# A three-stage attention and two-MLP kernel: warm-up matmuls planned with two activity levels, weight loads moved to GpSimd's queue

## The chip, the cores and the metric

The program runs on one core of a Trainium2 chip. The metric is device microseconds of one execution; the kernel before takes 969.86 us, the median of three runs (968.71 to 970.83). TensorE (PE in the profile) is the matrix engine, VectorE (DVE) and ScalarE (ACT) work on vectors, SyncE (SP) issues DMAs, and GpSimd (POOL) does nothing before but set four constants.

## The reference

Inputs are q, k, v of 4 batches, 8 heads, 576 positions and head size 64. The attention output is the sum of two softmax attentions: one on means over groups of 4 positions, and one in a band of 7 positions:

```python
out_d = sm_attn(q_d, k_d, v_d)                 # 144 pooled positions, dense
out_up = np.repeat(out_d, factor, axis=2)      # factor = 4
mask = np.abs(pos[:, None] - pos[None, :]) < factor
scores = np.where(mask, scale * np.matmul(q, k.transpose(0, 1, 3, 2)), -1e9)
out_local = softmax(scores) @ v
x = (out_up + out_local)                       # as 2304 tokens x 512
h = x @ w_in;  g = np.maximum(h, 0) + alpha * np.minimum(h, 0);  x = g @ w_out
h = x @ w_in2; g = np.where(h > 0, h, np.exp(np.minimum(h, 0)) - 1); out = g @ w_out2
```

Both MLPs are 512 to 2048 to 512. The weights arrive as 64-bit floats, and every MLP product is computed as three products of high and low parts.

## The kernel before, in words

The program is written out by a planner that runs when the kernel is built. It keeps a small clock of its own (class `_Clock`: an estimated time for each engine, and how many columns TensorE has streamed in each stretch of `TICK`), and it lets some hundred generator threads (`th_...`) place their next instruction when the estimated times allow it. What comes out is one fixed instruction order for each engine. The chip runs each engine's list in order and waits by semaphores; the estimates play no part there. All instructions pass through the helper at L231, so every row of the profile reads L231 and the tiles tell what it is.

The MLP runs in slots. A slot is one group of 288 tokens (384 in layer 2) and one block `f` of 128 hidden units: 12 matmuls with the input weights `wi` (`mm_in`), then the activation (`n`, `r`, `gh`, `gl`), then 12 matmuls with the output weights `wo` (`out1`). The first run of slots, 0 to 9, is group 0 with `f` = 0 to 9; slots 10 to 25 are group 1 with all 16 blocks; 26 to 31 finish group 0. Before a weight block can be used, it is loaded raw (512 KB, tile `raw`), and converted by two ACT and four DVE instructions (`cp`, `cw`, `wi` or `wo`); in layer 1, this is `th_conv(1, k)` for the 32 blocks in the order wi0, wo0, wi1, and so on.

The attention of batch 0, first half of the positions, comes before slot 0: banded blocks per pair of heads (`th_dense`, tiles `dP`), pooled attention (`P`, `pt`, `od`), the sum `x`, and its parts `xh` and `xl`. The second half (u = 1) follows while the slots already run, and it goes through DRAM: the score blocks `ss` are written to `scr`, their band is read back as `s`, a softmax on DVE gives `a`, which is written to the diagonal of `pscr` and read back as `pp`; TensorE transposes `pp` and multiplies it with `vb`. Batch 1 goes the same way in two halves. `pscr` holds zeros first, from two DMAs of 702 KB. `xsp` is a copy of x in DRAM.

All DMAs are issued by SP, in one order. The weight loads of layer 1 come from `th_ldw(1)`: load k waits in the planner until block k - 4 is converted (`PF`), and for the tiles whose memory it takes over. `run_while` is where the planner has nothing to place: it moves its time on by 100 ns, and when `quiet()` says that TensorE has streamed too few columns in the present stretch it places a warm-up matmul (tile `warm`, 128x128 by 256 columns, its result unused).

Of the kernel before, what the change touches and what calls it, by code (L numbers as in the profile page):

```python
# [7 lines left out]
F32 = mybir.dt.float32  # L8
# [9 lines left out]
NP = H // 2  # L18
# [19 lines left out]
T0 = 600.0  # L38
QB, QK = 64, 70
QO = 0, 64, 128, 192, 224  # L40
MORE = 1.0
LIM, EARLY, ECONV, DLA = 1300.0, 700.0, 200.0, 2000.0
PB, FB, RB, PF, CS = 1000.0, 300.0, 300.0, 4, 6
OS, OP, OPS, OSD, OSO, OAV, OX = 5, 15, -8, 6, 0, 10, -5
# [11 lines left out]


class _Clock:
    TICK, BUSY = 10240 / 3, 2640.0
    LAG = {("ACT", "DVE"): 142.0, ("ACT", "PE"): 194.0, ("ACT", "SP"): 145.0, ("DVE", "ACT"): 128.0,  # L60
           ("DVE", "DVE"): 127.0, ("DVE", "PE"): 179.0, ("DVE", "SP"): 120.0, ("PE", "ACT"): 197.0,
           ("PE", "DVE"): 196.0, ("PE", "SP"): 189.0, ("DMA", "SP"): 900.0, ("DMA", "ACT"): 907.0,
           ("DMA", "DVE"): 907.0, ("DMA", "PE"): 1003.0, ("ACT", "ACT"): 140.0}
    MANY = {"ACT": 70.0, "DVE": 93.0, "SP": 50.0, "PE": 0.0}

    def __init__(self):
        self.cols = {}
        self.t = dict.fromkeys(("PE", "ACT", "DVE", "SP", "DMA"), 0.0)
        self.t["SP"] = 560.0
        self.hw = 0.0  # L70
        self.seen = {}
        self.share = 1.0
        self.uses, self.bar, self.slots, self.count = {}, {}, {}, {}
        self.cur = self.ctx()
# [5 lines left out]
    def pe(self, t, cost, share):  # L80
        k = int(t / self.TICK)
        while cost > 0.0:
            slow = 1.0 if self.cols.get(k - 1, 0.0) >= self.BUSY else 2.0
            part = min(cost, ((k + 1) * self.TICK - t) / slow)
            self.cols[k] = self.cols.get(k, 0.0) + part * 2.4 * share
            t, cost, k = t + part * slow, cost - part, k + 1
        return t

    def quiet(self):
        k = int(self.t["PE"] / self.TICK)  # L90
        return self.cols.get(k, 0.0) < MORE * self.BUSY

    def span(self, ap):
        dims = [(abs(int(a)), int(n)) for a, n in ap.ap]
# [21 lines left out]
    def deps(self, eng, outs, ins):  # L116
# [13 lines left out]
        for src, e in last.items():  # L130
            if e > self.seen.get((eng, src), 0.0):
                self.seen[eng, src] = e
                n += 1
                t = max(t, e + self.LAG.get((src, eng), 0.0))
        return t + (self.MANY[eng] if n > 1 else 0.0)

# [26 lines left out]
            n, want = n * k, want * k  # L163
        return n * (8 if ap.dtype == U64 else 4)

    def dma(self, out, in_):
        outs, ins = [self.span(out)], [self.span(in_)]
        n = int(out.shape[0]) * _free(out) * (8 if out.dtype == U64 else 4)
        piece = min(self.run(out), self.run(in_))
        cost = max(n / 360 * (2 if piece < 512 else 1), n / piece / 16 * 7)  # L170
        self.t["SP"] = max(self.t["SP"], self.deps("SP", outs, ins))
        self.hw = max(self.hw + 25, self.t["SP"]) + 450
        end = max(self.t["DMA"], self.hw + 650) + cost
        self.t["DMA"] = end
        self.note("DMA", outs, ins, end)
        c = self.cur
        c["t"] = max(c["t"], end + 900)
        c["on"] = "DMA"


def _free(ap):
    n = 1
    for d in ap.shape[1:]:
        n *= int(d)
    return n


class _Engine:
# [31 lines left out]
    def __getattr__(self, op):  # L220
        fn = getattr(self.eng, op)

        def call(*args, **kw):
            if op == "dma_start":
                self.clock.dma(kw["out"], kw["in_"])
            else:
                outs = [kw[k] for k in ("out", "accum_out") if k in kw] + list(args[:1])
                ins = [a for k, a in kw.items() if k not in ("out", "accum_out") and hasattr(a, "ap")]
                wait = 0.6 * int(kw["lhsT"].shape[1]) if op == "matmul" else 0.0
                self.clock.op(self.name, *self.cost(op, kw, args), outs, ins + list(args[1:]), wait)  # L230
            return fn(*args, **kw)  # L231
        return call
# [3 lines left out]
def fused_kernel(ctx: ExitStack, tc: tile.TileContext, qk, vt, vl, ql, kl, vb, w_in1, w_out1, alpha,  # L236
                 w_in2, w_out2, ident_d, mask_d, zero_d, vd, maskd_d, out):
    nc = tc.nc
    ck = _Clock()
    PE, ACT, DVE, SP = (_Engine(n, e, ck) for n, e in  # L240
                        (("PE", nc.tensor), ("ACT", nc.scalar), ("DVE", nc.vector), ("SP", nc.sync)))

    const = ctx.enter_context(tc.tile_pool(name="const", bufs=1))
    wp = ctx.enter_context(tc.tile_pool(name="w", bufs=1))
# [10 lines left out]
    maskb = const.tile([128, 5, QK], BF16, name="maskb")  # L255
    identb = const.tile([128, 128], BF16, name="identb")
    warm = const.tile([128, 4], BF16, name="warm")

    W = {}
    raw = {}  # L260
# [51 lines left out]
    wsrc = {(1, "i"): w_in1, (1, "o"): w_out1, (2, "i"): w_in2, (2, "o"): w_out2}  # L312

    def load_w(key):
        ly, nm, f = key
        if wide:
            raw[key] = wp.tile([128, 512], U64, tag=f"w{nm}{f}", name=f"raw{nm}{f}")
            SP.dma_start(out=raw[key], in_=wsrc[ly, nm][f])

    gs = {}  # L320
    cp = {}
# [19 lines left out]
    st = {}  # L341
# [408 lines left out]
    def finish(*key):  # L750
        done[key] = ck.cur["t"]
# [80 lines left out]
    def run_while(cond):  # L832
        while cond():
            now[0] = max(now[0], ck.t["PE"])
            while not (cons() | pe(RB)) and cond():
                now[0] += 100
                while WARM and keep[0] is not None and ("S", 0, NP - 1, 0) in done and ck.t["PE"] < now[0] - 50 and ck.quiet():
                    at(now[0] - 100)
                    PE.matmul(out=keep[0][:, 0:256], lhsT=warm[:, 0:1].to_broadcast([128, 128]),
                              rhs=warm.unsqueeze(1).to_broadcast([128, 64, 4]),  # L840
                              start=True, stop=True)
                assert now[0] < 5e6, [(t["p"], t["w"]) for t in threads]
# [4 lines left out]
    def fill(budget):  # L847
        now[0] = max(now[0], ck.t["PE"])
        cons()
        pe(budget)  # L850

    def tick():
        sync()
        pe(PB)
        ck.cur = ck.ctx()
# [370 lines left out]
    def th_ldw(ly):  # L1226
        for k, it in enumerate(items):
            if ly == 2:
                yield "key", "fr", (2,) + it
            else:  # L1230
                if PT0 <= k < PP0:
                    yield "key", "pav", 0, k - PT0, 0
                elif PP0 <= k < V0:
                    yield "key", "pav", 0, k - PP0, 0
                elif V0 <= k < SH0:
                    yield "key", "sv", 0, k - V0
                elif k >= QK0:
                    yield "key", "dav", (k - QK0) // 2, (1,)
                    for u in range(2):
                        yield "key", "smm", 0, (k - QK0) // 2, u  # L1240
                if k >= PF:
                    yield "key", "cv", 1, k - PF
            yield ("DMA",)
            load_w((ly,) + it)
            finish("ld", (ly,) + it)
            ck.cur["t"] = now[0]
# [185 lines left out]
    with tc.manual_schedule():  # L1432
# [32 lines left out]
        spawn(th_soft0(0, 1), -10, 0)  # L1465
        spawn(th_vb(0, 1), UV, 0)
        spawn(th_ldw(1), 0)
        for k in range(2 * NF):
            spawn(th_conv(1, k), k / CS, early=ECONV)
# [29 lines left out]
        for s in range(NS1 + NS2):  # L1499
            slot[0] = s if s else -1  # L1500
            ly, g, f, first, last, i = seq[s]
# [3 lines left out]
            if s == T7:  # L1505
                assert all(t["p"] < -50 for t in threads), [t["w"] for t in threads]
                pA.__exit__(None, None, None)
                pC = tc.tile_pool(name="pC", bufs=1)
                cp["pool"] = pC.__enter__()
                tokens.update({"x2": [0.0], "x2s": [0.0, 0.0], "cp": [0.0] * 2, "cw": [0.0] * 2, "os": [0.0] * 4})  # L1510
                spawn(th_ldw(2), 0)
                for k in range(2 * NF):
                    spawn(th_conv(2, k), 2 + k / 100)
                for gg in range(NG2):
                    spawn(th_x2(gg), gg)
# [5 lines left out]
            key = (ly, "i", f)  # L1521
# [124 lines left out]
```

## Time and profile before

| | |
|---|---|
| median of 3 runs | 969.86 us (968.71 to 970.83) |
| the profiled execution | 970.52 us, span 968.7 us |
| busy, share of the span | PE 97%, LDWEIGHTS 89%, DVE 62%, ACT 49%, POOL 0% |
| mean granted clock | 0.974 |
| warm-up matmuls | 60 |
| DMA | 86.17 MB, one queue in use by the program |

The profile gives an instruction's start from the first instruction's; "granted clock" is the share of full speed that TensorE was given in a stretch, 1.00 for 2.4 GHz and 0.50 for 1.2 GHz. Matmul durations overlap, so a busy PE is not at its peak. Times on SP are those of issuing a DMA, not of its landing.

### The profile page before, as it was taken

How to read it: one execution, taken by the hardware profiler on the slowest of the kernel's cores; microseconds unless marked ns; L12 is line 12 of the kernel's file. 1: busy time of each engine (PE TensorE's matmuls, PEld its weight loads, DVE VectorE, ACT ScalarE, POOL GpSimd, SP SyncE). 2: the span in 40 equal slices, each digit the busy share in tenths (PEclk: the TensorE clock that was granted, in tenths of full speed). 3: DMA queues.
4: the chain of work that ended last, by engine and by line, in shares of the span. 5: the costliest groups of instructions: out<-in, count | busy, mean ns of one | idle time of the engine just before them, and what ended most of it. 6: DMA issues, size and time to landing. Idle time of an engine off the chain costs nothing.

```text
span 968.7 us, 16336 instructions
## 1 busy us (share of the span) xinstructions
PE 938.5 (97%) x6428; PEld 866.0 (89%) x6428; DVE 599.5 (62%) x1253; ACT 471.3 (49%) x1200; POOL 0.2 (0%) x4
## 2 busy tenths in 40 slices
PE   5978999899999999999999999999999999999998
PEld 3767889799999899999999999989999999998997
DVE  5778998645959789899638999732322322322222
ACT  5575678555432572332326677644443433433433
POOL 0000000000000000000000000000000000000000
PEclk9687999989999999999999999999999999999999
DMA  9277762534111523100207950003100100000000
GB/s 291 93 247 228 240 222 52 102 110 160 50 31 54 167 70 90 33 19 37 82 1 238 377 195 33 1 1 98 55 12 1 66 1 1 33 1 1 33 1 32
DMA packets 60933, 86.17 MB, mean 89 GB/s; under 512 B 29279, under 2 KB 40415, under 8 KB 60599
## 3 DMA queue, kind: packets, MB, share of 16 engines
q1 hardware_dynamic: 60857, 85.14, 28.0%
q8 instruction: 50, 0.82, 0.4%
q14 instruction: 26, 0.21, 0.1%
HBM read 69.93 MB, written 16.63 MB: 89 GB/s over the span
## 4 chain that ended last, share of the span: by engine, by line
PE 89%; DMA 6%; ACT 2%; DVE 2%; issue 1%; SPq 1%; ACTq 0%
PE bank L231 89%; DMA scr<-ss 2%; DMA s<-scr 1%; DMA qk<-in_qk_dram 1%; DMA pp<-pscr 1%; DMA pscr<-a 1%; SPq L231 1%; ACT dP L231 0%; DVE cw L231 0%; ACT ss L231 0%; ACT cp L231 0%; ACT P L231 0%; DVE s L231 0%; ACT n L231 0%; DVE cp L231 0%
## 5 line engine op out<-in xcount | busy, mean ns | idle before, releaser
L231 PE MATMUL bank<-xh,wi 128*128 128x288 f32 x1024 | 240.6, 304 | 3.6 <-DVE wi L231 2.8
L231 ACT ACTIVATE n<-bank 128x288 f32<-128x288 f32 (+1 forms) x224 | 99.4, 444 | 290.7 <-PE bank L231 290.5
L231 PE MATMUL bank<-gh,wo 128*128 128x288 f32 x1024 | 237.1, 302 | 1.2 <-ACT ys L231 1.2
L231 PE MATMUL bank<-x2h,wi 128*128 128x384 f32 x768 | 211.2, 337 | 0.0
L231 PEld LDWEIGHTS bank<-xh,wi 128*128 128x128 f32 x1024 | 176.4, 191 | 8.6 <-DVE wi L231 3.9
L231 PEld LDWEIGHTS bank<-gh,wo 128*128 128x128 f32 x1024 | 174.4, 190 | 6.3 <-issue 2.9
L231 PE MATMUL bank<-wo,gh 128*128 128x512 f32 x576 | 179.0, 392 | 0.0
L231 DVE SCALAR_TENSOR_TENSOR r<-n,bank 128x384 f32<-128x384 f32 x96 | 53.1, 554 | 195.0 <-ACT n L231 194.9
L231 ACT ACTIVATE gh<-r 128x288 fp32r<-128x288 f32 (+1 forms) x224 | 106.8, 477 | 100.2 <-DVE r L231 99.7
L231 PE MATMUL bank<-xl,wi 128*128 128x288 f32 x512 | 152.9, 299 | 0.0
L231 PE MATMUL bank<-gl,wo 128*128 128x288 f32 x512 | 151.8, 297 | 0.0
L231 DVE TENSOR_TENSOR gl<-r,gh 128x288 fp32r<-128x288 f32 (+1 forms) x224 | 111.4, 498 | 60.8 <-ACT gh L231 59.2
L231 PEld LDWEIGHTS bank<-x2h,wi 128*128 128x128 f32 x768 | 140.3, 188 | 3.9
L231 PE MATMUL bank<-x2l,wi 128*128 128x384 f32 x384 | 128.9, 336 | 0.0
L231 PEld LDWEIGHTS bank<-wo,gh 128*128 128x128 f32 x576 | 106.8, 188 | 18.2
L231 PE MATMUL bank<-wo,gl 128*128 128x512 f32 x288 | 113.8, 395 | 0.0
L231 DVE SCALAR_TENSOR_TENSOR r<-n,nal,bank 128x288 f32<-128x288 f32 x128 | 65.2, 509 | 53.1 <-ACT n L231 52.5
L231 PEld LDWEIGHTS bank<-xl,wi 128*128 128x128 f32 x512 | 98.0, 191 | 0.0
L231 PEld LDWEIGHTS bank<-gl,wo 128*128 128x128 f32 x512 | 97.3, 190 | 0.0
L231 PEld LDWEIGHTS bank<-x2l,wi 128*128 128x128 f32 x384 | 72.1, 188 | 3.8
L231 PEld LDWEIGHTS bank<-wo,gl 128*128 128x128 f32 x288 | 54.0, 187 | 11.5
L231 ACT ACTIVATE n<-n 128x384 f32<-128x384 f32 x96 | 50.4, 525 | 3.1
(101 smaller groups left out, 895.6 us busy)
## 6 DMA issues: line engine op xcount, KB each, us to landing
rawi<-in_w_in_dram SPq DMA_DIRECT2D x32, 512.0 KB
rawo<-in_w_out_dram SPq DMA_DIRECT2D x32, 512.0 KB
qk<-in_qk_dram SPq DMA_DIRECT2D x12, 582.0 KB
yT<-ys SPq DMA_DIRECT2D x32, 144.0 KB
out_dram<-os SPq DMA_DIRECT2D x18, 256.0 KB
vl<-in_vl_dram SPq DMA_DIRECT2D x4, 960.0 KB
vv<-in_vt_dram SPq DMA_DIRECT2D x12, 288.0 KB
kls<-in_kl_dram SPq DMA_DIRECT2D x12, 288.0 KB
```

The lines of the kernel that those rows point to most:

```text
L231: return fn(*args, **kw)
```

## The change

The planner's model of TensorE's clock gets a memory. Before, a stretch was taken as slow when the stretch before it had fewer than `BUSY` (2640) columns. Now a fast stretch stays fast at `BUSY` columns, a slow one becomes fast only after `RISE` (3500), and the first `FREE` (6) stretches are taken as fast; `quiet()` asks for warm-ups up to the level of the present state. The weight loads are issued by GpSimd, and the limit of four loads ahead of the conversions is dropped in favour of one wait: before its first load GpSimd copies one column of the last `v` tile of batch 0, which makes it wait until that tile has landed.

```diff
 class _Clock:
-    TICK, BUSY = 10240 / 3, 2640.0
+    TICK, BUSY, FREE, RISE = 10240 / 3, 2640.0, 6, 3500.0
...
     def pe(self, t, cost, share):
         k = int(t / self.TICK)
         while cost > 0.0:
-            slow = 1.0 if self.cols.get(k - 1, 0.0) >= self.BUSY else 2.0
+            slow = 1.0 if self.fast(k) else 2.0
...
+    def fast(self, k):
+        while len(self.gear) <= k:
+            n = len(self.gear)
+            need = self.BUSY if n and self.gear[-1] else self.RISE
+            self.gear.append(n < self.FREE or self.cols.get(n - 1, 0.0) >= need)
+        return self.gear[k]
+
     def quiet(self):
         k = int(self.t["PE"] / self.TICK)
-        return self.cols.get(k, 0.0) < MORE * self.BUSY
+        return self.cols.get(k, 0.0) < (self.BUSY if self.fast(k) else self.RISE)
...
-    def dma(self, out, in_):
+    def dma(self, out, in_, eng="SP"):
...
+        if eng == "SP":
+            self.hw = max(self.hw + 25, self.t["SP"]) + 450
+            end = max(self.t["DMA"], self.hw + 650) + cost
+        else:
+            self.t[eng] += 1000
+            end = max(self.t["DMA"], self.t[eng] + 650) + cost
...
-            SP.dma_start(out=raw[key], in_=wsrc[ly, nm][f])
+            GP.dma_start(out=raw[key], in_=wsrc[ly, nm][f])
...
-                if k >= PF:
-                    yield "key", "cv", 1, k - PF
+                if not k:
+                    yield "key", "ldv", NP - 1
+                    nc.gpsimd.tensor_copy(out=pace, in_=st["vv", 0, NP - 1][:, 0:1])
```

Since the planner places everything by its estimates, the order on all engines shifts. Warm-up matmuls are 52 instead of 60: 30 before slot 0 (22 before), 8 between slots 0 and 1 (10), 9 after slot 1 (18), 5 later (10).

PE, before, between the transposes of batch 0's banded blocks (`dP_197` is pair 1, `dP_220` pair 2; bank_71 takes the warm-ups):

```order
L231 MATMUL bank_72<-ident,dP_197 70x128 x4
L231 MATMUL bank_69<-ident,dP_197 70x128
L231 MATMUL bank_73<-ident,dP_220 70x128 x4
L231 MATMUL bank_66<-ident,dP_220 70x128
L231 LDWEIGHTS warm
```

PE, now, at the same place (`dP_166` is pair 0, `dP_206` pair 1, `dP_257` pair 2):

```order
L241 MATMUL bank_72<-dP_166,vd_124 64x64 x8
L241 MATMUL bank_72<-dP_166,vd_124 64x32 x2
L241 MATMUL bank_73<-ident,dP_206 70x128 x4
L241 MATMUL bank_67<-ident,dP_206 70x128
L241 LDWEIGHTS warm
L241 MATMUL bank_71<-warm 128x256
```

The last two rows come three times before the transposes of `dP_257` follow. So the product of pair 0's block with `vd` has moved up ahead of the later transposes, and three warm-ups stand between two pairs that adjoined.

SP, before, from the last loads of batch 0 to the second half's band `s_777`:

```order
L231 DMA vd_141<-in_vd_dram 70x640
L231 DMA rawi_230<-in_w_in_dram 128x512
L231 DMA rawo_273<-in_w_out_dram 128x512
L231 DMA rawi_275<-in_w_in_dram 128x512
L231 DMA rawo_288<-in_w_out_dram 128x512
L231 DMA rawi_485<-in_w_in_dram 128x512
L231 DMA xsp<-x 128x1152
L231 DMA mask<-in_mask_dram 128x182
L231 DMA pscr_98<-in_zero_dram 12x14982
L231 DMA pscr_97<-in_zero_dram 12x14982
L231 DMA scr_1_94<-ss 72x624 x2
L231 DMA rawo_592<-in_w_out_dram 128x512
```

SP, now, from the same load on:

```order
L241 DMA vd_142<-in_vd_dram 70x640
L241 DMA xsp<-x 128x1152
L241 DMA mask<-in_mask_dram 128x182
L241 DMA pscr_99<-in_zero_dram 12x14982
L241 DMA pscr_98<-in_zero_dram 12x14982
L241 DMA scr_1_95<-ss 72x624 x4
L241 DMA s_784<-scr_1_95 72x32x7
L241 DMA pscr_99<-a 72x32x7
L241 DMA pp<-pscr_99 72x624 x4
L241 DMA vb<-in_vb_dram 78x2048
```

The weight loads are gone from between, and so are, before the band is read, the loads of `vb`, `qk` and `vv`. GpSimd, which had no such rows before, now has all 64 loads; its list begins so:

```order
L1255 COPY pace<-v_3_138 128x1
L241 DMA rawi_292<-in_w_in_dram 128x512
L241 DMA rawo_294<-in_w_out_dram 128x512
L241 DMA rawi_319<-in_w_in_dram 128x512
L241 DMA rawo_332<-in_w_out_dram 128x512
L241 DMA rawi_349<-in_w_in_dram 128x512
L241 DMA rawo_370<-in_w_out_dram 128x512
```

Eight loads have nothing to wait for but the copy; the next eight wait for the products of batch 0's banded blocks, whose memory they take, and loads 25 to 32 for the pooled attention of the second half.

SP, before, in batch 1 (`pscr_97` holds the first half, `pscr_98` the second; `s_2264` is the second half's band):

```order
L231 DMA pscr_97<-a 72x32x7
L231 DMA s_2264<-scr_1_96 72x32x7
L231 DMA pp<-pscr_97 72x624
L231 DMA scr_1_92<-ss 72x4x78
L231 DMA qk<-in_qk_dram 128x1164
L231 DMA vv<-in_vt_dram 128x576
L231 DMA pp<-pscr_97 72x624
L231 DMA pscr_98<-a 72x32x7
L231 DMA pp<-pscr_97 72x624
```

SP, now, at that place (`pscr_98` is the first half, `pscr_99` the second, `s_2192` the second half's band):

```order
L241 DMA scr_1_97<-ss 72x624
L241 DMA s_2192<-scr_1_97 72x32x7
L241 DMA qk<-in_qk_dram 128x1164
L241 DMA vv<-in_vt_dram 128x576
L241 DMA pscr_98<-a 72x32x7
L241 DMA pscr_99<-a 72x32x7
L241 DMA pp<-pscr_98 72x624
```

Both halves' softmax results are now written before the first `pp` is read. On DVE the conversions keep their places: the tenth `wi` has nine `wo` ahead of it in both orders, and the band's softmax of batch 0 stands after the fourth `wi` in both.

## Rows read from the trace of the kernel before

**Rows 1.** Page, busy us, share of the span and instructions by engine.

```profile
PE 938.5 (97%) x6428; PEld 866.0 (89%) x6428; DVE 599.5 (62%) x1253; ACT 471.3 (49%) x1200; POOL 0.2 (0%) x4
```

**Rows 2.** Windows: stretch, length, busy us by engine, granted clock, DMA share, GB/s.

```profile
21.40:41.90 20.50, 20.11 (x171) 14.62 (x171) 15.52 (x40) 10.59 (x39) 0.00 (x0) 0.50 0.17 65
52.10:55.50 3.40, 3.40 (x27) 2.64 (x26) 1.90 (x5) 3.37 (x13) 0.00 (x0) 0.50 0.82 266
69.20:72.60 3.40, 3.40 (x26) 2.56 (x26) 3.23 (x11) 2.69 (x10) 0.00 (x0) 0.50 0.36 84
76.00:89.60 13.60, 11.11 (x67) 10.14 (x67) 10.17 (x19) 6.65 (x16) 0.00 (x0) 0.50 0.82 251
89.60:182.00 92.40, 90.17 (x809) 83.87 (x809) 81.40 (x166) 66.41 (x183) 0.00 (x0) 1.00 0.53 162
192.00:198.90 6.90, 5.09 (x25) 5.12 (x26) 1.80 (x5) 4.28 (x15) 0.00 (x0) 0.51 0.57 170
198.90:960.00 761.10, 760.43 (x4902) 712.87 (x4902) 443.98 (x912) 338.48 (x791) 0.00 (x0) 1.00 0.20 64
```

**Rows 3.** Chain that ended last: start us, us, what.

```profile
23.37 18.55 PE bank L231 x157
...
54.52 7.38 DMA scr<-ss
...
61.97 5.31 DMA s<-scr
...
70.84 6.27 DMA pscr<-a
77.13 2.73 DMA pp<-pscr
...
79.91 21.98 PE bank L231 x206
```

**Rows 4.** Waits of PE, 41.9 to 110 us: us, times, longest.

```profile
PE bank L231 <- DVE wi L231: 2.8, 4, 1.1
...
PE bank L231 <- DMA pp<-pscr: 2.3, 1, 2.3
```

**Rows 5.** Timeline of PE: the last wait for converted weights.

```profile
109.25 0.54 PE L231 MATMUL bank<-xh,wi 128*128 128x288 f32 x2 [1.07 <-DVE wi L231]
```

**Rows 6.** Windows of DVE alone: busy us, granted clock, DMA share, GB/s.

```profile
5.30:41.00 35.70, 26.30 (x73) 0.73 0.54 174
41.00:67.30 26.30, 19.38 (x43) 0.92 0.84 270
67.30:109.20 41.90, 36.87 (x75) 0.80 0.74 231
```

**Rows 7.** The same windows for warm-up instructions alone, 21.4 to 41.9 us.

```profile
21.40:41.90 20.50, 5.22 (x19) 2.33 (x19) 0.00 (x0) 0.50 0.17 65
```

**Rows 8.** SP's timeline: start, us to issue, what.

```profile
15.55 0.33 SPq L231 DMA_DIRECT2D rawi<-in_w_in_dram  x1
40.06 0.33 SPq L231 DMA_DIRECT2D xsp<-x  x1
...
185.19 4.20 SPq L231 DMA_DIRECT2D pp<-pscr  x1
```

**Rows 9.** Windows: DMA at full rate, and DMA idle.

```profile
17.07:20.48 3.41, 2.33 (x19) 1.41 (x16) 3.24 (x12) 2.98 (x17) 0.00 (x0) 1.00 1.02 362
27.31:30.72 3.41, 3.41 (x38) 2.23 (x35) 2.76 (x9) 1.36 (x7) 0.00 (x0) 0.50 0.00 0
```

**Rows 10.** Groups by line and form, 0 to 110 us: busy us, mean ns.

```profile
L231 DVE TENSOR_SCALAR cp<-cp 128x512 uint32<-128x512 uint32 x21 | 8.8, 419 | 0.0
```

**Rows 11.** Timeline of PE, 180 to 194 us: batch 1's blocks `pp`.

```profile
183.34 0.78 PE L231 MATMUL bank<-ident,pp 72*78 72x72 f32 x8 [0.99 <-DMA pp<-pscr]
...
189.99 0.67 PE L231 MATMUL bank<-ident,pp 72*78 72x72 f32 x8 [0.96 <-DMA pp<-pscr]
...
193.81 1.15 PE L231 MATMUL bank<-ident,pp 72*78 72x72 f32 x8 [2.30 <-DMA pp<-pscr]
```

More of the change, by code (lines that the diff above doesn't have):

```diff
@@ L40 @@
 QO = 0, 64, 128, 192, 224
-MORE = 1.0
 LIM, EARLY, ECONV, DLA = 1300.0, 700.0, 200.0, 2000.0
@@ L63 @@
            ("DMA", "DVE"): 907.0, ("DMA", "PE"): 1003.0, ("ACT", "ACT"): 140.0}
-    MANY = {"ACT": 70.0, "DVE": 93.0, "SP": 50.0, "PE": 0.0}
+    MANY = {"ACT": 70.0, "DVE": 93.0, "SP": 50.0, "PE": 0.0, "GP": 50.0}
     def __init__(self):
-        self.cols = {}
-        self.t = dict.fromkeys(("PE", "ACT", "DVE", "SP", "DMA"), 0.0)
+        self.cols, self.gear = {}, []
+        self.t = dict.fromkeys(("PE", "ACT", "DVE", "SP", "DMA", "GP"), 0.0)
         self.t["SP"] = 560.0
@@ L170, in dma @@
         cost = max(n / 360 * (2 if piece < 512 else 1), n / piece / 16 * 7)
-        self.t["SP"] = max(self.t["SP"], self.deps("SP", outs, ins))
-        self.hw = max(self.hw + 25, self.t["SP"]) + 450
-        end = max(self.t["DMA"], self.hw + 650) + cost
+        self.t[eng] = max(self.t[eng], self.deps(eng, outs, ins))
+        if eng == "SP":
[4 more added lines that the diff above has]
+            end = max(self.t["DMA"], self.t[eng] + 650) + cost
         self.t["DMA"] = end
@@ L224, in call @@
             if op == "dma_start":
-                self.clock.dma(kw["out"], kw["in_"])
+                self.clock.dma(kw["out"], kw["in_"], self.name)
             else:
@@ L239, in fused_kernel @@
     ck = _Clock()
-    PE, ACT, DVE, SP = (_Engine(n, e, ck) for n, e in
-                        (("PE", nc.tensor), ("ACT", nc.scalar), ("DVE", nc.vector), ("SP", nc.sync)))
+    PE, ACT, DVE, SP, GP = (_Engine(n, e, ck) for n, e in
+                            (("PE", nc.tensor), ("ACT", nc.scalar), ("DVE", nc.vector), ("SP", nc.sync),
+                             ("GP", nc.gpsimd)))
     const = ctx.enter_context(tc.tile_pool(name="const", bufs=1))
@@ L257, in fused_kernel @@
     warm = const.tile([128, 4], BF16, name="warm")
+    pace = const.tile([128, 1], F32, name="pace")
     W = {}
```

## The prediction

> **What bounds the kernel now.** I read the page's busy shares first, then windows with the granted clock, the chain, PE's waits, and DVE alone. PE is busy 97% of the span [rows 1]. From 198.9 us on it is busy 760.43 of 761.10 us at full clock, and from 89.6 to 182 us 90.17 of 92.40 [rows 2]. Neither part has anything to give, so what this change can win or lose lies before 89.6 us and between 182 and 199 us. There the granted clock falls to 0.50, which is 1.2 GHz, four times, for 20.5, 3.4, 3.4 and 13.6 us, and once more for 6.9 us [rows 2].
>
> A slow PE alone is not the bound, though. In the slots up to 9, PE waits for converted weights four times, the last time at 109.25 us [rows 4, 5]: there the conversions on DVE set the pace. DVE's ledger is therefore the one to keep. From 5.3 us to the last `xl` of slot 0 at 41.0 us it works 26.3 of 35.7 us (9.4 idle); to the band's softmax at 67.3 us 19.4 of 26.3 (6.9 idle); to the tenth `wi` at 109.2 us 36.9 of 41.9 (5.0 idle) [rows 6]. Its work in these three parts is the same after the change, since the order keeps the conversions' places. The kernel can become faster by as much of the 21.3 us of idle time as goes, until PE is the bound by itself.
>
> **The change part by part.**
>
> *A, warm-ups before slot 0.* From 23.4 us the chain is PE alone for 18.55 us [rows 3], at half clock although PE was busy 20.11 of 20.50 us; 5.22 us of that were 19 warm-ups, 0.27 us each, and they did not bring the clock back for 20 us [rows 2, 7]. Real work was 14.9 us at half clock, so 7.5 at full. The 30 warm-ups now cost 30 x 0.14 = 4.2 us at full clock. With the clock held PE needs 11.7 us where DVE needs 15.5 [rows 2], so DVE becomes the bound and the stretch shrinks by at most 20.5 - 15.5 = 5.0 us. With the clock not held, eight more warm-ups at 0.27 us cost 2.2 us. The warm-ups now stand closer together and the planner asks more of a slow stretch, so I lean to the first and take a gain of 4 us: DVE will still wait on ACT and PE somewhere.
>
> *B, the band's way through DRAM.* Before, SP's queue is the weights' queue too. The fourth `scr` write took 7.38 us from issue to landing and the read of `s` 5.31 [rows 3]; `vb` and weights were issued just ahead. Now nothing but the chain's own DMAs stands there. Against that, loads no longer pause: before, the DMA engines stood still between 24 and 40 us, when `xsp` was at the head of SP's queue [rows 8, 9]; now GpSimd issues on as memory comes free. A load takes 512 KB / 362 GB/s = 1.45 us at the rate of [rows 9], so 24 loads fill 35 us from about 18 us on, and run into the `scr` and `s` transfers of 44 to 67 us. Between all 6.9 us of idle time gone and 5 us lost (the price is worked out with the rivals), I take a gain of 2 us, nearest to the queueing that the 7.38 us show over the 5.31.
>
> The trace has one program queue, so it shows no sharing between two. The Trainium skill, "DMA: Bandwidth & Descriptors", sections "Issuing engines are not separate DMA queues" and "Queues, rings and completion order", says that transfers issued by different engines run on the same 16 DMA engines, which take packets from their queues in turn, and that a second issuer saves issue time alone. By that, B alone gives nothing or a loss, and the total would be 2 us higher; no run here shows it yet.
>
> *C, up to the tenth `wi`.* From 76 to 89.6 us PE ran at half clock, busy 11.11 us, after waiting for `pp` for 2.3 us [rows 2, 4]; at full clock that is 5.6 us. DVE idles 5.0 us in this part. Bounds are 0 and 5.0; I take 3, since the second half's `x` sums stand some ten us of DVE work further back now, which covers the read of `pp`.
>
> *D, batch 1.* PE waits 0.99, 0.96 and 2.30 us for three `pp` blocks [rows 11], and the clock is low for 6.9 us after it, of which 5.09 busy [rows 2]: 4.2 + 2.5 = 6.7 us lost. In the new order there are 21 more MLP matmuls between the last score blocks and the first `pp`; at 761.1 us / 4902 = 0.155 us they cover 3.3 us. But both halves' `pscr` writes now stand ahead of the first `pp`, and before, the read behind the second write took 4.20 us to issue [rows 8] and landed 8.6 us after its issue. One long wait replaces three short ones. Bounds: 6.7 gained, 4 lost (8.6 less 3.3, less the 0.99 that the first wait was); I take 0.
>
> *E, issuing on GpSimd.* No row shows its cost. SP's issues take from 0.33 us to 4.20 [rows 8]. The tenth `wi` is load 19: at 0.33 us an issue nothing waits, at 4.2 us it goes out at 18 + 80 = 98 us, too late by some us for its conversion. I go by the lower end, since the long issue stood in a queue full of small pieces. What it can disturb is DVE. The copies `cp` take 0.419 us [rows 10]; 24 loads that each hold one up by its length would cost 10 us, loads that hold up none cost 0. `cp` fills 8.8 of 110 us, so a random load meets one in 8% of cases: 24 x 0.08 x 0.42 = 0.8 us. I take 1 us lost, which is near the lower end because most of DVE's instructions here are of other forms.
>
> The Trainium skill, "SBUF - State Buffer", section "SBUF: two separate sides", holds that DVE and GpSimd lock each other out of a shared port for a whole instruction when DVE runs in a two-port mode, and that loads issued from GpSimd then wait for their descriptors. By that rule the loads are late by up to one `cp` each, which the earlier start covers; the sum by it is the same to 1 us.
>
> *The rest.* Layer 2's 32 loads move to GpSimd too; PE there is busy all the time [rows 2] and I price them at nothing. If that cover were gone, PE would wait as in [rows 5], 1 us a block.
>
> Sum: 4 + 2 + 3 + 0 - 1 = 8 us off the profiled execution's 970.5 us, 962.5; that execution lies 0.7 us above the median of 969.86, so 962.
>
> **The rivals.** *All of it comes.* The clock holds, the chain is early, and D goes too: 5.0 + 6.9 + 5.0 of DVE's idle time, limited by PE's own needs to about 11, and 6 from D: 953. For it speaks that PE has 20 us at half clock to give before 89.6 us; against it that DVE's waits on ACT and PE are many and small. Chance 0.15.
>
> *The clock does not hold.* The warm-ups don't do what they are for: PE falls to half clock near 21 us again and stays there until slot 0. A costs 2 us, B and C give 3 to 4 at most since the weights are there earlier: 969. For it: 19 warm-ups in a stretch that was busy 98% left the clock low. Chance 0.18.
>
> *The loads crowd out the band.* This is the slower side, one mechanism: 24 loads (35 us) and the chain's own 2.8 MB (by the tiles' sizes 576 KB of `xsp`, 91 of mask, 1404 of zeros, 704 of `scr`; at 362 GB/s 8 us) begin at 18 us, so the DMA engines have work until 61 us. The band's read is 2304 pieces of 28 bytes (72 x 32 runs in the order), and before it took 5.31 us with little beside it. If its pieces wait in turn with whole weight rows it can't end before the loads do; with `vb` and later loads behind that it lands near 72 instead of 67.3 us, DVE stands still in front of its softmax, PE idles, the clock falls, and A's gain is lost there. The `pp` reads suffer in the same way: 974. It decides from the landing of `s`: later than 68 us and the change loses. For it: the DMA engines were busy 0.84 of this part already [rows 6]. Chance 0.22.
>
> **How the numbers follow.** My forecast, 962, has 0.45, with a range of its own of 956 to 968. A measurement of this kernel can tell about 0.2%, 1.9 us, from no change. Faster than that (below 967.9): nearly all of the forecast, the first rival and a third of the second: 0.43 + 0.15 + 0.06 + 0.02 = 0.66. Slower (above 971.8): most of the third and a fifth of the second: 0.19 + 0.04, 0.23. The same: 0.11. The range reaches from a little below the first rival to the third: 951 to 975.
>
> **What would show it.** A: no stretch at 0.50 longer than two of the short ones between 21 us and slot 0, and slot 0's last `xl` near 37 us. B: `s` lands near 61 us; DMA never idle between 18 and 55 us. C: the tenth `wi` at about 100 us. D: one wait for `pp` of 3 to 6 us instead of three. E: `cp` on DVE at 0.42 us, or longer. The forecast is wrong if `xl` comes after 40 us, if the band's softmax begins after 65 us, or if PE idles for more than 8 us in batch 1.

## The result, and the profile after

| | before | after |
|---|---|---|
| median | 969.71 us (968.71 to 970.83, 4 runs) | 980.59 us (980.01 to 982.46, 4 runs) |
| the profiled execution | 970.52 us | 980.49 us, span 978.7 us |

The ratio is 1.0122, with a 95% interval of 1.0104 to 1.0139: the changed kernel is slower by 10.9 us, where 962 was forecast with a range up to 975.

The page's busy time by engine (us, share of the span, instructions), to be held against [rows 1]:

```profile
PE 935.1 (96%) x6429; PEld 864.4 (88%) x6429; DVE 598.7 (61%) x1253; ACT 472.8 (48%) x1200; POOL 35.1 (4%) x69
```

PE is busy 3.4 us less than before in a span that is 10.0 us longer: the loss is idle time. The windows of the changed kernel, with the columns of [rows 2], cut where its granted clock changes:

```profile
32.90:39.70 6.80, 6.59 (x49) 5.04 (x47) 4.58 (x9) 3.39 (x8) 2.39 (x5) 0.50 0.41 126
53.40:60.20 6.80, 6.45 (x31) 5.76 (x32) 5.89 (x11) 4.87 (x13) 2.58 (x5) 0.50 1.00 390
70.45:94.35 23.90, 12.66 (x67) 10.86 (x68) 17.00 (x38) 12.17 (x32) 2.37 (x4) 0.50 0.54 123
94.35:182.00 87.65, 87.27 (x806) 81.05 (x804) 80.11 (x167) 65.58 (x182) 0.00 (x0) 1.00 0.38 101
189.90:200.20 10.30, 9.48 (x57) 8.36 (x58) 3.90 (x8) 3.23 (x9) 0.00 (x0) 0.50 0.48 123
200.20:960.00 759.80, 757.38 (x4917) 710.50 (x4915) 443.91 (x912) 342.15 (x806) 17.53 (x32) 1.00 0.21 66
```

Before slot 0 the clock is low for 6.8 us instead of 20.5. How short that stretch is differs between executions: of the nine traces with this same list of PE (this one and eight of the experiments below), three have some 6.8 us there and six some 13.6, the changed kernel's second trace (e12) among them, while the two with the planning of before (e2, e9) have 20.5. From e12:

```profile
28.00:41.50 13.50, 11.53 (x82) 8.37 (x79) 10.35 (x24) 6.95 (x21) 4.69 (x9) 0.50 0.67 226
```

So the warm-ups shorten it, but not always by as much as this trace shows. From 70.45 us on the clock is low for 23.9 us, and PE is busy half of that. In sum no clock is won: the stretches at 0.50 shown here add up to 47.8 us, and those of [rows 2] do too. What comes before the 23.9 us is in the chain that ended last, the DMA pieces of 40 to 80 us (start us, us, what):

```profile
41.60 10.15 DMA scr<-ss
...
54.91 5.57 DMA scr<-ss
60.61 13.36 DMA s<-scr
```

The read of `s` went out 1.4 us earlier than in [rows 3] and took 13.36 us instead of 5.31. It was the same read, 2304 pieces of 28 bytes; what had changed was beside it. The DMA queues from 60 to 74 us (packets, MB, share of the 16 engines' time):

```profile
q0 software_dynamic: 1004, 3.61, 70.0%
q1 hardware_dynamic: 2316, 0.06, 9.7%
```

q0 holds GpSimd's weight loads, q1 the band. 0.06 MB of the band spread over the time of 3.61 MB of weight rows. GpSimd's timeline shows where these came from (start, us to issue):

```profile
17.10 0.18 POOL L1255 COPY pace<-v 128x1 f32<-128x1 f32 x1 [16.66 <-DMA v<-in_vt_dram]
17.22 0.66 POOL L241 DMA_DIRECT2D rawi<-in_w_in_dram  x1
...
59.06 0.53 POOL L241 DMA_DIRECT2D rawi<-in_w_in_dram  x1 [1.00 <-PE bank L241]
60.95 0.53 POOL L241 DMA_DIRECT2D rawo<-in_w_out_dram  x1 [1.35 <-DMA rawi<-in_w_in_dram]
64.04 0.53 POOL L241 DMA_DIRECT2D rawi<-in_w_in_dram  x1 [2.57 <-PE bank L241]
64.66 0.53 POOL L241 DMA_DIRECT2D rawo<-in_w_out_dram  x1
```

Nine of its loads go out between 51.33 and 64.66 us, in the middle of the band's way. What the late band does to DVE and PE, as their waits from 40 to 110 us (us, times, longest), DVE first:

```profile
DVE s L241 <- DMA s<-scr: 10.7, 1, 10.7
```

```profile
PE bank L241 <- ACT P L241: 9.5, 1, 9.5
PE bank L241 <- ACT ss L241: 3.5, 1, 3.5
PE bank L241 <- DMA pp<-pscr: 2.8, 1, 2.8
```

DVE stands in front of the band's softmax for 10.7 us, since its list is fixed. Work of the pooled attention is queued behind it, so PE stands 9.5 us for `P`, and meanwhile the clock falls. DVE alone, in the stretches of [rows 6], and then the tenth `wi`:

```profile
5.30:41.00 35.70, 28.50 (x77) 0.90 0.86 288
...
41.00:67.30 26.30, 17.92 (x39) 0.87 0.99 375
...
67.30:109.20 41.90, 31.68 (x67) 0.71 0.57 152
```

```profile
112.25 0.68 DVE L241 SCALAR_TENSOR_TENSOR wi<-cw,wi 128x512 fp32r<-128x512 f32 x1
```

DVE has done 2.2 us more work by 41 us than in [rows 6], but idles 10.2 instead of 5.0 us in the third part; the tenth `wi` is ready at 112.9 instead of 109.2 us. SP's timeline gives the rest:

```profile
36.90 0.35 SPq L241 DMA_DIRECT2D xsp<-x  x1
...
60.61 0.31 SPq L241 DMA_DIRECT2D s<-scr  x1
77.25 0.30 SPq L241 DMA_DIRECT2D pscr<-a  x1
83.62 9.78 SPq L241 DMA_DIRECT2D pp<-pscr  x4
93.45 0.36 SPq L241 DMA_DIRECT2D vb<-in_vb_dram  x1
```

And in batch 1 PE's timeline has one long wait where [rows 11] have three short ones:

```profile
190.72 1.15 PE L241 MATMUL bank<-ident,pp 72*78 72x72 f32 x8 [4.55 <-DMA pp<-pscr]
```

### The profile page after: what moved, and what is told of

Its sections match the earlier page's. It is cut to its first block, busy times and chain, and to the rows that moved or that the text cites. A ratio compares the mean times of both kernels' runs of the same rounds, so it can differ in the third digit from the quotient of the medians.

```text
span 978.7 us, 16380 instructions
## 1 busy us (share of the span) xinstructions
PE 935.1 (96%) x6429; PEld 864.4 (88%) x6429; DVE 598.7 (61%) x1253; ACT 472.8 (48%) x1200; POOL 35.1 (4%) x69
## 4 chain that ended last, share of the span: by engine, by line
PE 46%; issue 45%; DMA 4%; DVE 2%; ACT 2%; SPq 0%; POOL 0%; POOLq 0%; ACTq 0%; DVEq 0%
PE bank L241 46%; DMA scr<-ss 2%; DMA s<-scr 1%; ACT dP L241 1%; DMA yT<-ys 1%; ACT P L241 1%; DMA rawi<-in_w_in_dram 0%; DVE cw L241 0%; DMA ident<-in_ident_dram 0%; DVE qk L241 0%; DVE wi L241 0%; ACT ss L241 0%; DVE cp L241 0%; ACT cp L241 0%; DVE x L241 0%
## 5 line engine op out<-in xcount | busy, mean ns | idle before, releaser
L241 PE MATMUL bank<-xh,wi 128*128 128x288 f32 x1024 | 244.8, 307 | 4.1 <-ACT wi L241 2.1
```

## The experiments

Theory "crowding": the loads on the second queue share the DMA engines with the band's small pieces. Rivals: the new instruction order itself costs the time ("order"), issuing from GpSimd does ("GpSimd"), or the missing limit of four does ("limit"). The experiments ran on other chips, where the kernel before took 964.4 to 965.1 us (medians, single runs 958.7 to 969.8). So ratios to the kernel before, taken in the same runs, are compared, not times.

| run | loads from, limit in the planner, what else | ratio | 95% interval |
|---|---|---|---|
| e12_after | GpSimd, no limit: the changed kernel again | 1.0118 | 1.0094 to 1.0141 |
| e1_clock_only | SP, limit | 0.9965 | 0.9947 to 0.9983 |
| e16_clock_again | the same | 0.9972 | 0.9952 to 0.9992 |
| e6_one_queue | SP, no limit | 1.0072 | 1.0048 to 1.0097 |
| e2_pool_only | GpSimd, no limit, clock model of before | 1.0131 | 1.0096 to 1.0165 |
| e3_hold | GpSimd, no limit, loads from the 17th on held until `s` is there | 1.0140 | 1.0111 to 1.0169 |
| e4_paced | GpSimd, limit as a wait on the chip | 1.0167 | 1.0135 to 1.0199 |
| e5_hold_pp | as e3, held until the second `pp` is there | 1.0080 | 1.0061 to 1.0098 |
| e7_hold_swap | as e5, batch 1's second write moved back | 1.0064 | 1.0043 to 1.0084 |
| e10_vb | as e7, `vb` early | 1.0032 | 1.0014 to 1.0050 |
| e11_all | as e10, layer 2's loads on SP | 1.0016 | 0.9998 to 1.0033 |
| e8_l2_sp | the changed kernel, layer 2's loads on SP | 1.0097 | 1.0077 to 1.0117 |
| e9_copies | the kernel before, eight copies beside the band | 1.0090 | 1.0060 to 1.0119 |
| e13_limit | GpSimd, limit | 1.0127 | 1.0102 to 1.0152 |
| e14_limit_hold | as e13, loads from the 15th on held until the second `pp` | 1.0004 | 0.9981 to 1.0027 |
| e15_close | as e14, layer 2's loads on SP | 0.9994 | 0.9973 to 1.0016 |

**Each half alone.** e1_clock_only:

```diff
-            GP.dma_start(out=raw[key], in_=wsrc[ly, nm][f])
+            SP.dma_start(out=raw[key], in_=wsrc[ly, nm][f])
...
-                if not k:
-                    yield "key", "ldv", NP - 1
-                    nc.gpsimd.tensor_copy(out=pace, in_=st["vv", 0, NP - 1][:, 0:1])
+                if k >= PF:
+                    yield "key", "cv", 1, k - PF
```

> The changed kernel's clock model alone: the weight loads are issued by SP again, with the limit of four loads ahead. Theory 'crowding' (the weight rows of the second queue share the DMA engines with the 28-byte pieces of the band's read, which took 13.4 us instead of 5.3, and everything behind it is late): without the second queue the read of s takes 5 to 7 us from its issue and s lands by 68 us; the gain before slot 0 of about 2 us stays: 967 us (964 to 970). Rival 'order' (the instruction order and the warm-ups that the new model makes cost the time, whoever issues the loads): 977 to 981 us.

e2_pool_only, the changed kernel with the clock model of before:

```diff
-            slow = 1.0 if self.fast(k) else 2.0
+            slow = 1.0 if self.cols.get(k - 1, 0.0) >= self.BUSY else 2.0
...
-        return self.cols.get(k, 0.0) < (self.BUSY if self.fast(k) else self.RISE)
+        return self.cols.get(k, 0.0) < self.BUSY
```

> The weight loads on GpSimd alone, without a limit ahead, under the clock model of before. Theory 'crowding': the read of s is long again, 10 us or more, and there is no gain before slot 0: 978 to 984 us. Rival 'order': the order is nearer to that of before, 968 to 972 us. Rival 'GpSimd' (issuing from GpSimd costs by itself, whatever the loads run beside): 976 to 984 too, but with a read of s of about 5 us.

The clock model alone makes the kernel faster by 0.3%. The loads on GpSimd alone make it slower by as much as the whole change does (the intervals of e2 and e12 overlap). e2's read of `s` takes 10.94 us in its chain, e1's 4.07. Both are as the first theory has it. The next two runs, which should have confirmed it, did not.

**Holding the loads back.** e3_hold keeps the list of every engine but GpSimd:

```diff
+            if ly == 1 and items.index((nm, f)) >= 16 and ("sr", 0, 1) not in done:
+                ck.dma(raw[key], wsrc[ly, nm][f], "GP")
+                held.append((raw[key], wsrc[ly, nm][f]))
+                return
...
+        if (b, u) == (0, 1):
+            nc.gpsimd.tensor_copy(out=pace[0:BLK], in_=st["s", 0, 1][:, 0, 0, 0:1])
...
+            for o, i in held:
+                nc.gpsimd.dma_start(out=o, in_=i)
```

> The changed kernel with the order of every engine except GpSimd word for word unchanged; GpSimd's 17th and later loads wait until s of batch 0 has landed (a copy of one column of s stands before them). Theory 'crowding': the read of s takes 5 to 7 us, s lands by 68 us, DVE's wait for it falls from 10.7 to under 5 us, PE does not idle 9 us there, and the time falls by 4 to 7 us, to 974 to 977 (the loss in batch 1 and the small ones later stay). Rival 'order' or 'GpSimd': 979 to 982, and the read of s as long as before the edit.

It gave nothing, against the expectation. Its chain says why (start us, us, what):

```profile
69.37 19.25 DMA pscr<-a
88.63 2.58 DMA pp<-pscr
```

DVE no longer waits for `s`, but the held loads start as soon as it has landed (nine are issued from 63.04 to 68.48 us), and the next transfer of 28-byte pieces, the write of `a`, takes 19.25 us instead of 6.27 [rows 3]. The crowding was moved one transfer on. e4_paced makes the limit a real wait, by a copy of one column of block k - 4 once it is converted:

```diff
+                if k >= PF:
+                    z = (1,) + items[k - PF]
+                    yield "key", "w", z
+                    nc.gpsimd.tensor_copy(out=pace, in_=W[z][:, 1, 0:1].bitcast(F32))
```

> The changed kernel with the limit of four loads ahead put back for GpSimd in layer 1: before load k GpSimd copies one column of the converted block k - 4. The loads stay on their own queue. Theory 'crowding': at most four loads are ahead, so that the read of s takes 5 to 9 us and the time is 968 to 975 us, better than the changed kernel by 5 us or more. Rival 'GpSimd': 979 or more. Rival 'order': 977 or more.

`s` takes 5.90 us here, and the kernel is slower still. ACT's waits from 40 to 120 us:

```profile
ACT cp L241 <- DMA rawi<-in_w_in_dram: 8.7, 5, 5.5
ACT cp L241 <- DMA rawo<-in_w_out_dram: 6.4, 4, 4.3
```

Now the conversions wait 15.1 us for the raw blocks. The planner reckoned with these copies, so the order of PE, DVE and ACT changed as well, and this run alone can't tell the two apart. In the kernel before the limit was an order in the planner only, and no wait on the chip. e5_hold_pp is e3 with the copy taken from the second `pp` instead of `s`:

```diff
+        if (b, p, u) == (0, 1, 1):
+            nc.gpsimd.tensor_copy(out=pace[0:BLK], in_=st["pp", 0, 1, 1][:, 0, 0, 0:1])
```

> As e3_hold (order of every other engine unchanged), but GpSimd's 17th and later loads wait until the second block pp of batch 0 has been read back, not only until s has landed. In e3_hold the nine held loads started together when s had landed, and the next transfer of 28-byte pieces, the write of a to pscr, took 19.25 us instead of 6.3. Theory 'crowding': now s takes 5 to 6 us, the write of a 5 to 7, and PE's wait for pp is under 4 us instead of 12.8; the held loads still come in time for the ninth wi (needed at about 98 us). Ratio to the kernel before 1.002 to 1.006, against 1.0140 of e3_hold and 1.0122 of the changed kernel. Rival 'order' (what is lost lies in the sequence of PE, DVE and ACT): 1.010 or more, with PE idle elsewhere. Rival 'late loads': DVE and PE wait for raw blocks at 85 to 110 us, 1.010 or more.

The ratio falls to 1.0080, less than expected. The whole way of the band is short now, the first `pp` is asked for at 73.22 instead of 83.62 us, and PE's waits from 40 to 110 us name the next thing:

```profile
PE bank L241 <- DMA vb<-in_vb_dram: 7.7, 1, 7.7
PE bank L241 <- ACT ss L241: 4.4, 1, 4.4
```

**One queue.** e6_one_queue undoes the issuing engine alone, and leaves the limit out: in the diff of e1 the two lines added for `PF` are missing.

> The changed kernel with the loads issued by SP, still without the limit of four: PE's order is the same word for word, DVE's and ACT's differ at 15 and 10 places, and the loads stand in SP's order where the planner places them, ahead of and between the band's transfers. Theory 'crowding by the second queue': a read that stands behind loads in one queue waits for those ahead of it and is not mixed with those behind it; the read of s takes 4 to 7 us, the write of a 5 to 7, and the ratio is 0.998 to 1.005. Rival 'limit' (it is the missing limit that puts too many loads ahead of the band, in whatever queue): the read of s takes over 9 us here too, ratio 1.008 or more. Rival 'order': 1.010 or more with s of 4 to 7 us.

1.0072, between the theories' numbers. The chain:

```profile
57.39 4.15 DMA s<-scr
65.07 7.64 DMA pscr<-a
73.56 6.86 DMA pp<-pscr
82.49 11.48 DMA vb<-in_vb_dram
```

In one queue `s` is short without any limit, but `vb` comes last and PE waits for it (4.7 us, and 4.3 us for `pp`). So a part of the loss needs no second queue: without the limit, and with all loads on SP as in e1, the ratio is 0.0107 above e1's. Without the limit the planner's order has `vb` behind the four `pp`. In the code, the thread that loads `vb` has a lower priority than the weight loads, and both place a DMA only while the planner's DMA time is at most 2000 ns ahead; that unlimited loads use this up is read from the code and not shown by a run.

**The places behind `pp`.** e7_hold_swap adds to e5 that SP issues batch 1's second write of `a` behind two reads:

```diff
+        if (b, u) == (1, 1) and ("pr", 1, 1, 0) not in done:
...
+            late.append(1)
...
+        if (b, p, u) == (1, 1, 0) and late:
...
+            nc.sync.dma_start(out=diag(pscr[1]), in_=st["a", 1, 1].rearrange("q h k x -> q (h k) x"))
```

> As e5_hold_pp, and in batch 1 the second half's write of a to pscr moved on SP from ahead of the first pp to behind the second. Before, PE stands still 3.4 us there and the granted clock is 0.50 for 10.2 us after it. Theory 'SP's order in batch 1 costs': PE's wait for pp after 180 us goes, and the ratio is 0.002 to 0.005 below that of e5_hold_pp. Rival: the second write is late now, the second half's pp comes 3 to 5 us later and PE waits there instead: same ratio as e5_hold_pp within 0.001.

0.0016 less than e5, smaller than the intervals. PE's longest wait for `pp` from 120 us on is 0.6 instead of 2.6 us, so the direction holds and the size stays open. e10_vb adds the load of `vb` ahead of the third `scr` write:

```diff
+        if ("S", 0, 0, 1) in done and ("vb", 0, 1) not in st:
+            st["vb", 0, 1] = Ap.tile([KW, 4, H, D], F32, tag="vl", name="vb")
+            nc.sync.dma_start(out=st["vb", 0, 1], in_=vb[0, :, 4:8])
```

> As e7_hold_swap, and the load of vb of batch 0, which in the changed kernel stands on SP behind the four reads of pp, goes out between the scr writes, as in the kernel before; no other order is changed. In e5_hold_pp and e7_hold_swap PE waited for it 7.7 and 5.5 us. Theory 'vb is the third part of the loss': that wait goes, and the ratio falls by 0.003 to 0.006, from 1.0064 to 1.000 to 1.0035. Rival 'conversions': DVE's conversions set the pace in that part and take the time back: 1.005 or more.

1.0032: PE's wait for `vb` is gone, as expected. The ratio is 0.0032 below e7's, on another chip and with intervals that just overlap. e8_l2_sp and e11_all issue layer 2's loads from SP, the first in the changed kernel, the second in e10:

```diff
+            if ly == 2:
+                ck.dma(raw[key], wsrc[ly, nm][f], "GP")
+                nc.sync.dma_start(out=raw[key], in_=wsrc[ly, nm][f])
+                return
```

> The changed kernel with layer 2's loads alone issued by SP; the planner's times and all other orders unchanged. In all kernels with the loads on GpSimd some 1.5 to 1.9 us are lost between slots 120 and 132, where layer 1's results (yT) go out through ACT and SP and the loads of layer 2 run; in e1_clock_only nothing is. Theory 'crowding', at a second place: ACT's and PE's wait there goes, and the ratio falls by 0.0015 to 0.002, to 1.010 to 1.011. Rival: SP's queue now blocks behind loads that wait for memory, and yT is as late or later: 1.012 or more.

> As e10_vb, and layer 2's loads issued by SP: everything that the runs so far name is put back, with the order of PE, DVE and ACT of the changed kernel word for word. If the four named places are the whole loss, this order is as good as that of e1_clock_only (0.9965): 0.996 to 1.001, and 0.001 to 0.002 below e10_vb. Rival: something is still unnamed: 1.002 or more.

Each is about 0.002 below its partner (e12, e10), twice the same sign, but within the intervals. By the ends of `gh` in the traces, the changed kernel loses 1.6 us against the kernel before between slots 120 and 132. In the changed kernel ACT's waits from 540 to 600 us have a row that neither the kernel before nor e8 has:

```profile
ACT ys L241 <- DMA yT<-ys: 1.7, 1, 1.7
```

e11_all misses its expectation and falls 0.0051 short of e1, with intervals that do not overlap. Its list of PE is the changed kernel's, and e1's is another; so in this order the four places are not all of it, and the rival "order", which here is what planning without the limit makes of PE's, DVE's and ACT's lists, may hold what is left. No run takes it apart.

**The price of the crowding by itself.** e9_copies is the kernel before, with traffic added and no order changed:

```diff
+            nc.gpsimd.tensor_copy(out=pace[0:BLK], in_=st["lastss"][:, 0, 0, 0:1])
+            for i in range(8):
+                nc.gpsimd.dma_start(out=dump[i][:, 0:512], in_=wsrc[2, "i"][i])
```

> The kernel before, every order unchanged on PE, DVE, ACT and SP; GpSimd copies one column of the last scr source tile and then issues eight copies of a 512 KB weight block from DRAM to DRAM, in pieces of 4 KB, whose result nothing uses. They run beside the last scr write and the read of s. It is the price of the crowding without the planner. Theory 'crowding': the read of s takes 9 us or more instead of 5.31, the wait for it and what follows grow by 4 to 10 us, ratio 1.004 to 1.010. Rival 'order': in the order of before the band has slack enough, and nothing changes: 0.998 to 1.002 with s landing as before.

```profile
64.05 12.57 DMA s<-scr
80.19 5.17 DMA pscr<-a
```

The read of `s` takes 12.57 us instead of 5.31, and the ratio is 1.0090: 4 MB of other traffic on the second queue at that place is enough to lose 9 us. Neither the planner nor the converted weights have a part in it.

> The changed kernel once more, so that it is compared with the kernel before in the same runs as the variants: ratio 1.012, within 1.010 to 1.0145, by both theories; its read of s 11 to 14 us again.

The changed kernel in the same runs gave 1.0118, with a read of `s` of 12.03 us.

**The fourth corner.** e13_limit is the changed kernel with the limit in the planner, which gives PE the list of e1 word for word. e14_limit_hold holds its loads as e5 does, from the 15th on; no other list changes.

```diff
+                if k >= PF:
+                    yield "key", "cv", 1, k - PF
```

> The changed kernel with the limit of four put back in the planner alone (load k is placed after block k - 4 is converted, without a wait on the chip); the loads stay on GpSimd. PE's order is that of e1_clock_only word for word, vb stands between the scr writes again and batch 1's first pp ahead of the second write of a. With e1_clock_only (SP, limit: 0.9965), e6_one_queue (SP, no limit: 1.0072) and the changed kernel (GpSimd, no limit: 1.0118) this is the fourth corner. Theory 'two losses that add': dropping the limit costs 0.0107 by the order on SP, the second queue 0.0046 by the crowding; so here the order is good and the crowding stays: 1.001 (0.998 to 1.005), the data of s 6 to 10 us long. Rival 'the limit paced the loads': with it the crowding goes too, 0.995 to 0.998, and s short. Rival 'crowding is the whole': 1.008 or more.

> As e13_limit, and GpSimd's 15th and later loads wait until the second block pp of batch 0 has been read back. The orders of PE, DVE, ACT and SP are those of e13_limit word for word. Theory 'two losses that add': the crowding goes, s takes 2 to 5 us, and the ratio is that of e1_clock_only, 0.995 to 0.999, below e13_limit by 0.002 to 0.006. Rival: the held loads are late for the conversions at 90 us, same as e13_limit or worse.

e13 answers against "two losses that add": 1.0127, no better than without the limit, though `vb` is early. Its DVE waits from 40 to 120 us:

```profile
DVE s L241 <- DMA s<-scr: 14.6, 1, 14.6
```

In e14 DVE has no wait in front of the softmax, which stands there 16.7 us earlier than in e13 (at 80.33 us):

```profile
63.62 0.38 DVE L241 SCALAR_TENSOR_TENSOR s<-s,mask 72x224 f32<-72x224 f32 x1
```

The two kernels differ in GpSimd's waiting copy alone, and by 0.0123 in the ratio, 12 us. The DMA records show the read itself. In e14 the 2304 pieces move from 60.64 to 62.21 us, 1.6 us, with no weight rows among them; the DMA queues from 60.60 to 62.25 us:

```profile
q1 hardware_dynamic: 2316, 0.06, 78.5%
```

In the kernel before they take 3.7 us, in e13 8.4 us with 1.9 MB of weight rows starting among them, and in the changed kernel 9.2 us with 2.0 MB. The last pair:

> As e14_limit_hold, and layer 2's loads issued by SP. The orders of PE, DVE and ACT stay word for word. e14_limit_hold was as far ahead of the kernel before as e1_clock_only up to slot 120 (8.78 and 8.76 us by the end of the gh of a slot) and lost 2.2 us from there to slot 132. If the first MLP's loads beside the band and layer 2's loads beside yT are the whole price of GpSimd's queue, this kernel is e1_clock_only's equal: 0.995 to 0.999, within 0.002 of e16_clock_again. Rival 'issuing from GpSimd has a price of its own': 0.003 or more above e16_clock_again.

> e1_clock_only once more, on the same chip and in the same runs as e15_close: the new clock model with all loads on SP under the limit. 0.9965 again, within 0.9945 to 0.9985.

e15 is 0.0022 above e16, between what was expected and the rival, with intervals that overlap: nearly all of the price of GpSimd's queue is in the two places named, and whether 2 us are left can't be told from these runs. e1_clock_only, the only version that beats the kernel before (by 0.3%, in two sets of runs), is the version to keep.

## Why the prediction was wrong

The step that failed is B: "Now nothing but the chain's own DMAs stands there", and the gain of 2 us taken from it. On SP's queue that was true. In the DMA engines the loads stood beside the chain, and `s` landed 6.7 us later than before (DVE's softmax at 74.0 instead of 67.3 us) where it was to land near 61. The choice was made "nearest to the queueing that the 7.38 us show over the 5.31", two rows with one queue each; the sentence above it has 24 loads that "run into the `scr` and `s` transfers", and DMA engines already busy 0.84 of the time were in [rows 6]. The prediction's own sign of being wrong came true, a softmax that begins after 65 us. The Trainium skill, "DMA: Bandwidth & Descriptors", section "Issuing engines are not separate DMA queues", holds that transfers started by different engines interleave on the same 16 DMA engines. The traces agree: the same read takes 4.15 us behind loads in one queue (e6) and 10.9 to 13.4 beside them in two (e2, e8, e9, e12, e13 and the changed kernel).

The rival "the loads crowd out the band" had the mechanism, the place, and a landing near 72 us (74.0), at a chance of 0.22. Its price was too small, 974 instead of 980.6. No sum stands behind the 974, so which part was short can't be told; that the `pp` reads suffer too did not come (PE waits 2.8 us for them, 2.3 before). e14 against e13 measures the crowding at 12 us in one order. In the changed kernel's own order taking it away gives only 0.0038 (e12 to e5), because `vb`, moved behind `pp` by the missing limit, is late too: a second loss hidden under the first. The forecast counted the going of `vb` from in front of the band as a help, and it had no term for the order that SP gets without the limit, which costs 0.0107 in one queue (e6 to e1).

Step by step. A, a gain of 4 us: the direction was right. `xsp` is issued at 36.90 instead of 40.06 us, 3.2 us; in seven more runs of the same list of PE it comes at 35.55 to 39.52, so 0.5 to 4.5 us. It did not hang on the clock, from which the term was argued: in e12 the clock was low for twice as long and `xsp` came at 36.16. C, a gain of 3: wrong, as it hung on B; the second half is late, PE is low for 23.9 us instead of 13.6, and from `xsp` to the end of the tenth `wi` it takes 76.0 instead of 69.1 us. D, nothing: one wait of 4.55 us came in place of three, as written, but the clock was low for 10.3 us after it instead of 6.9; the same kernel lost less in another run (e12: a wait of 2.73 us), so this term differs from run to run by more than I gave it. E, a loss of 1 us: `cp` on DVE is as long as in [rows 10], and an issue takes 0.53 us:

```profile
L241 DVE TENSOR_SCALAR cp<-cp 128x512 uint32<-128x512 uint32 x19 | 8.0, 419 | 0.0
```

All of DVE's 1253 instructions together take 598.7 us, 599.5 before [rows 1]. So no hold-up on DVE shows. Layer 2, priced at nothing: about 1.6 us, by ACT's wait for `yT`.

The sum was out by 18 us, +10 measured for -8. B and C make 12 of it: 6.9 lost for 5 gained. Some 2 us are D's (0.3 us more waiting, and half of 3.4 us more at half clock), 1.6 layer 2's and 0.8 what A fell short of; the 1 us of E that did not come counts against them. These are estimates from one pair of traces. The remaining 3 us or so come after batch 1's `pp`: by the ends of `gh` the loss is 5.3 us at slot 31 and 7.9 at slot 120. One piece of that can be named. The count of 52 warm-ups stated with the change leaves out nine; the trace has 61, and these nine stand among layer 1's slots, where the clock is at 1.00 anyway:

```profile
354.75 1.17 PE L241 MATMUL bank<-warm 128*128 128x256 bf16 x9
```

The rest is small pieces, and no run places them singly.

What I had not forecast either: where the clock model alone gains. PE's windows of 160 to 200 us (batch 1, columns as in [rows 2]), e1_clock_only and then the kernel before:

```profile
160.00:200.00 40.00, 39.02 (x383) 36.14 (x383) 24.50 (x57) 27.10 (x87) 0.00 (x0) 1.00 0.52 122
```

```profile
160.00:200.00 40.00, 35.76 (x310) 32.52 (x309) 23.01 (x56) 24.81 (x83) 0.00 (x0) 0.91 0.55 120
```

In e1 batch 1's first `pp` is read at 164.48 us, 16 us earlier than before (180.45), PE has no wait for it, and the clock stays up; e16 shows the same. By the ends of `gh`, e1 is 0.4 us ahead of the kernel before at slot 25 and 10.4 us at slot 31. The two traces are from different chips, though, and the later chips ran the kernel before 5 us faster as well; in e9, which has its order, batch 1 waits 2.0 us for `pp` and the clock is low for 3.4 us. So batch 1 is where these traces part, but the gain as a whole is the ratio's 0.0035, 3.4 us, and no run tells how much of it comes from there.

## What to carry to other kernels

A second issuing engine takes a wait out of one queue's order, and with it what kept bulk transfers off a short chain: look in the DMA rows at what will run beside the chain's small pieces, not only at what stands ahead of them. Bulk loads that run free want a stop at the chain's end, made by a copy of one column of the last tile of the chain; a stop in its middle moves the crowd to the next transfer. When a fix gives back less than its wait was long, look for what had been late beneath it.

## What the runs showed of the hardware

- A read of 2304 pieces of 28 bytes, 0.06 MB, took 3.6 to 5.3 us from issue to use behind loads in the same queue (e16, e1, e6, the kernel before), and 10.9 to 13.4 us beside 4 KB rows of a second queue. The pieces themselves moved within 1.5 to 1.6 us with nothing beside them (e5, e14), and within 6.9 to 9.2 us with 1.2 to 2.2 MB of such rows starting among them (e2, e9, e12, e13, the changed kernel). A write of as many such pieces with 5.2 MB of rows beside it took 19.25 us from issue to use (e3) instead of 5.1 to 7.6.
- PE's waits and the low clock after them differ between runs of one kernel: in batch 1 the changed kernel waited 4.55 us with 10.3 us at 0.50 in one profile, and 2.73 us with 3.4 us at 0.50 in the other:

```profile
188.40:191.80 3.40, 3.40 (x28) 2.95 (x27) 0.58 (x2) 0.64 (x3) 0.00 (x0) 0.50 0.75 266
```
